# Sums of weight quarters made on GpSimd during the attention, from each converted piece, and stored beside it

## The chip, the cores and the metric

The program runs on one core of a Trainium2 chip. The metric is the time of one execution on the device in microseconds. A core has TensorE (matrix products, "PE" in the profile; its weight loads are "PEld"), VectorE ("DVE"), ScalarE ("ACT"), GpSimd ("POOL") and SyncE ("SP", here the queue from which nearly all transfers are issued).

## The reference

Three blocks follow each other. The attention works on 8 batches with 8 heads, 576 positions and 64 features; the mixer and the MLP work on 8 x 576 positions of 512 features.

```
phi(x): p = x @ w_phi; p = p - max|p|; concat(exp(p), exp(-p))
attention: (phi(q) @ (phi(k)^T v)) / (phi(q) . sum phi(k) + 1e-6)
gate = sigmoid(causal 5-tap convolution of x, per feature)
x = (gate * (x @ w_val)) @ w_out
u = x + real(FFT over positions and features of x)
un = layer norm of u
out = u + relu(un @ w_ch1) @ w_ch2
```

The weights w_val, w_out, conv_w, w_ch1 (512 x 2048) and w_ch2 (2048 x 512) come as 64-bit floats and are converted to 32 bits on the chip.

## The kernel before

Three phases follow each other. The attention (to about 312 us) is written out by hand in steps (`run_attention`): 16 units of two heads each, five groups of positions per unit, 80 steps in all. In each step TensorE projects (pj), transposes (yt, xt), accumulates phi(k)^T v (kv) and applies it (nm); VectorE takes maxima from PSUM (m, L260) and subtracts them (y, L263); ScalarE takes the exponentials (ke, qe). Finished heads go to DRAM by SP's queue (x_scr<-xT, L362).

Beside these steps 21 weight pieces are converted (`convert`), 16 of them of the two MLP weights (`conv_mlp`). A piece is loaded (raw, L121), ScalarE converts the low word, VectorE makes three passes (L133, L134 and the scalar_tensor_tensor into mt), ScalarE makes the exponent (L137) and the sign (L139), and GpSimd multiplies twice (L140, L141) in place in mt, a buffer of which there are two. Two places later `done` issues the store of mt from SP's queue (L378). The places of one piece lie 0, 3, 4, 5, 6 and 8 steps after its start, and a piece starts every 3.1 steps on average. Small tables are loaded through a tile tab between these steps.

A piece of an MLP weight is four quarters of 128 x 256 (a21, a11, a12, a22). The MLP multiplies 2 x 2 blocks with seven products instead of eight, and needs for it four sums of these quarters besides: s22 = a21 + a22, s21 = a11 - a21, s11 = s22 - a11, s12 = a12 - s11. Slots 0 to 3 of the scratch s_scr hold the quarters, slots 4 to 7 the sums.

Mixing (312 to about 620 us) and MLP are not written out by hand. Functions note operations with their costs and keys (`o_tt`, `o_lo`, `o_dma`, ...), and a planner (`place_ops`) puts all of them in one order, with due times from the products backwards; operations marked "vp" may go to VectorE or to GpSimd, whichever the planner finds better. In the mixing, `note_sums` loads a piece back from DRAM into one buffer ws, makes the four sums in place on GpSimd and stores them; a table SUMS says after which products each of the 16 pieces is noted. When the attention's pools are closed, `open_mix2` opens the second mixing stage's tiles and clears some of them on GpSimd (L453): c256, r256, xr, rem. The mixing computes val (x @ w_val), the taps (acc), gv and gs (gated values), ge (their two parts), ps (w_out and the Fourier products), and two halves of a first layer norm (s, sl, A, T).

All operations issued through helpers carry L62, so rows are told apart by their tiles. Products are made of a high and a low part, so many operations come in pairs: ScalarE writes the high part, VectorE or GpSimd the rest (xh, ge, f, sl).

Of the kernel before, what the change touches and what calls it, by code (L numbers as in the profile page):

```python
# [9 lines left out]
F32 = mybir.dt.float32  # L10
# [13 lines left out]
NE = HS + 2  # L24
# [41 lines left out]
def attention_moe_mixer_kernel(  # L66
# [46 lines left out]
        mm(o, al, bh, start=False, stop=last)  # L113


    def convert(i, src, n, shape, halve, done):
        raw = P["xf"].tile([128, 1024, 2], I32, tag="xf", name="raw64")[:, 0:n]
        raw_k = raw.rearrange("p n t -> p (n t)").rearrange("p (k f) -> p k f", k=shape[0])
        if shape[0] == 8:
            for o in range(2):  # L120
                nc.sync.dma_start(out=raw_k[:, o::2], in_=src[o])  # L121
        else:
            nc.sync.dma_start(out=raw_k, in_=src)
        yield
        lo32, hi32 = raw[:, :, 0].bitcast(U32), raw[:, :, 1]
        a = P["xh"].tile([128, 2, 1024], I32, tag=f"x{i % 2}", name="cv")
        ex, lo = a[:, 0, 0:n], f32(a[:, 1, 0:n])
        sg = lo
        mt = stg.tile([128, 1024], I32, tag="mt", name="mt")[:, 0:n]
        w = f32(mt)  # L130
        nc.scalar.activation(out=lo, in_=lo32, func=ACTF.Copy, scale=2.0 ** -32)
        yield
        nc.vector.tensor_scalar(out=mt, in0=hi32, scalar1=0xFFFFF, scalar2=0x4B000000, op0=ALU.bitwise_and, op1=ALU.bitwise_or)  # L133
        nc.vector.tensor_scalar(out=ex, in0=hi32, scalar1=0x7FF00000, scalar2=None, op0=ALU.bitwise_and)  # L134
        vec.scalar_tensor_tensor(out=w, in0=w, scalar=-7340032.0, in1=lo, op0=ALU.add, op1=ALU.add)
        yield
        nc.scalar.activation(out=ex, in_=ex, func=ACTF.Relu, scale=8.0, bias=ebias[:, int(halve):int(halve) + 1])  # L137
        yield
        nc.scalar.activation(out=sg, in_=hi32, func=ACTF.Sign)  # L139
        nc.gpsimd.tensor_tensor(out=w, in0=w, in1=f32(ex), op=ALU.mult)  # L140
        nc.gpsimd.tensor_tensor(out=w, in0=w, in1=sg, op=ALU.mult)  # L141
        yield
        done(w.rearrange("p (k f) -> p k f", k=shape[0]))
        yield
# [3 lines left out]
    def later(k, *at):  # L148
        def get():
            t = late[k]  # L150
            for i in at:
                t = t[i]
            return t
        return Late(get)
# [48 lines left out]
    y_p = pool(early, "y", 2, side=R)  # L203
    stg = pool(early, "stg", 2, side=R)
    vraw_p = pool(early, "vraw", 2, side=R)
    ps_pj = pool(early, "ps_pj", 2, PSUM, side=R)
    ap1 = pool(att, "ap1", 1)
    qe_p = pool(att, "qe", 4)
# [164 lines left out]
    def slices(i, j, q):  # L373
        return s_scr[i][j // (i + 1)][q, :, j % (i + 1)].rearrange("q p o f -> p q (o f)")

    def conv_mlp(n, j, i):
        def done(t):
            nc.sync.dma_start(out=slices(i, j, slice(0, 4)), in_=t.rearrange("p (q o) f -> p q (o f)", o=2))  # L378
        s = (w_ch1, w_ch2)[i][j].bitcast(I32).rearrange("o p (q f) -> o p q f", q=4)
        return convert(n, s, 1024, (8,), False, done)  # L380

    def note_sums(n):
        i, j = wsteps[n]
        t = later("ws")
        a21, a11, a12, a22 = (t[:, k] for k in range(4))
        k21, k11, k12, k22 = keys = [("ws", k) for k in range(4)]
        o_dma([(t, slices(i, j, slice(0, 4)))], [], keys, 512)
        o_tt("p", a22, a21, a22, ALU.add, 256, [k21, k22], [k22])
        o_tt("p", a21, a11, a21, ALU.subtract, 256, [k11, k21], [k21])
        o_tt("p", a11, a22, a11, ALU.subtract, 256, [k22, k11], [k11])  # L390
        o_tt("p", a12, a12, a11, ALU.subtract, 256, [k12, k11], [k12])
        o_dma([(slices(i, j, slice(4, 8)), t)], keys, [("s", i, j)], 512)

    def conv_taps(i):
        def done(t):
# [2 lines left out]

    def put_table(dst, src):
        r, n = src.shape  # L400
        t = stg.tile([128, 580], F32, tag="tab", name="tab")
        nc.sync.dma_start(out=t[0:r, 0:n], in_=src)
        yield
        hi_act(dst, t[0:r, 0:n])
        yield
# [12 lines left out]

    def open_mix():
        p = pool(gx, "g0", 1, side=R)  # L420
        ws = pool(vx, "ws", 1, side=R)
        psv = pool(vx, "psv", 1, PSUM, side=R)
        psa = pool(vx, "psa", 1, PSUM, side=R)
        for g, q in enumerate((p, P["g1"])):
            for i in range(2):
                late["ge", g, i] = q.tile([128, 4, 2, NE], F32R, tag=f"g{i}", name="ge")
        for i in range(2):
            late["pv", i] = psv.tile([128, NE + 2], F32, name=f"val{i}")
            late["gv", i] = P["g"].tile([128, NE], F32, tag="gv", name="gv")
            late["gs", i] = P["g"].tile([128, 2, NE], F32, tag="gs", name="gs")  # L430
        late["ws"] = ws.tile([128, 4, 256], F32, name="ws")
        late["pa"] = psa.tile([128, 2, 512], F32, name="acc")

    def open_mix2():
# [20 lines left out]
    def open_last():  # L455
# [4 lines left out]
        for i in (4,):  # L460
            late["ps", i] = ps.tile([128, 512], F32, name=f"ps{i}")
        open_mlp()

    wsteps = [(i, j) for j in range(NJ) for i in range(2)]

    def load_x(b):
        t = P["xf"].tile([128, 4, S + 4], F32, tag="xf", name="xf")
# [213 lines left out]
    def note_weights(c, n, first=[]):  # L681
        per = (7 * NJ, 7 * NJ // 2)[c]
        t, r = divmod(n, per)
        if t == len(BLOCKS):
            return
        j, i = divmod(r, 7)
        s = (f"r{c}", n % RING[c])
        w = later(s)
        hk, lk = s + (0,), s + (1,)
        cols = (256, 512)[c]  # L690
        h, l = (w[:, k].rearrange(("p k f -> p (k f)", "p n k f -> p (n k f)")[c]) for k in range(2))
        q = SLOT[ORDER[c][i]]
        src = s_scr[c][j][q].rearrange("p n k f -> p (n k f)")
        o_dma([(f32(l), src)], [("s", c, x) for x in ((j,), (2 * j, 2 * j + 1))[c] if q > 3] + first + (over(s) if c == 0 and n < RING[0] else []), [lk], (128, 256)[c])
        o_hi(h, f32(l), cols, [lk], [hk])
        o_lo(K["w"], l, f32(l), h, cols, [lk, hk], [lk])

# [251 lines left out]
    def note_W(b, c):  # L949
        gh, gl = (later(("ge", b % 2, k)) for k in range(2))  # L950
        w = int(b == NB - 1)
        t = later(("x2", w))
        fs, f = tl["fs"], [later(("f", i)) for i in range(2)]
        for a in range(2):
            k, p = next(ring)
            p = p[:, 0:NE]

            def prod(e, a=a, p=p):
                for kk in range(4):
                    ws = slice(c * 128, (c + 1) * 128)  # L960
                    mm3(p, (wo[0][:, kk, ws], wo[1][:, kk, ws]), (gh[:, kk, a], gl[:, kk, a]), kk == 0, kk == 3)
            op("m", 0, prod, [("ge", b % 2, kk, i) for kk in range(4) for i in range(2)] + ["wo"], [k] + [("done", "W", c, a)] * (b == NB - 2), 12 * 0.134)
            if c >= 2:
                o_tt("v", fs[:, a], t[:, c - 2, a], p, (ALU.add, ALU.subtract)[a], NE, [k, ("x2", w, c - 2, a)], [("fs", a)])
            if c == 2 and a == 0:
                r = later(("xr", b % 2))
                o_hi(r[0:1], p[0:1], NE, [k], [("xr", b % 2, 0)])
                o_lo("v", r[32:33], p[0:1], r[0:1], NE, [k, ("xr", b % 2, 0)], [("xr", b % 2, 1)])
            o_act(t[:, c, a], p, ACTF.Copy, NE, [k] + [("s",) + wsteps[-1]] * w, [("x2", w, c, a)])
        if c >= 2:  # L970
            c0 = c - 2
            fk = [("fs", 0), ("fs", 1)]
            o_hi(f[0][:, c0], fs, 2 * NE, fk, [("f", c0, 0)])
            o_lo(K["t_lo"], f[1][:, c0], fs, f[0][:, c0], 2 * NE, fk + [("f", c0, 0)], [("f", c0, 1)])
        if c == 2:
            q0 = 32 * (b % 4)
            o_act(later("r256")[q0:q0 + 1], t[0:1, 2], ACTF.Copy, 2 * NE, [("x2", w, 2, 0), ("x2", w, 2, 1)], [("r256", b % 4)])
# [79 lines left out]
    def note_mix():  # L1057
        rings = [[(("ps", i), later(("ps", i))) for i in range(n)] for n in (4, 5)]
        nonlocal ring
        ring = cycle(rings[0])  # L1060
        sums = iter(range(len(wsteps)))
        SUMS = [(1, 0, 1, 0, 1)] * 5 + [(1, 0, 0, 0, 0), (0,) * 5]

        def add_sums(n):
            for i in range(n):
                k = next(sums, None)
                if k is not None:
                    in_place(note_sums, k)

        ln0 = chain(ln_first(0), ln_first(1))  # L1070
        tail = note_tail()
        next(tail)
# [4 lines left out]
        for b in range(NB - 1):  # L1077
            note_x(b + 1)
            for i, c in enumerate((0, 2, 1, 3)):
                if i < 3:  # L1080
                    note_taps(b + 1, i)
                    note_V(b + 1, i)
                note_W(b, c)
                add_sums(SUMS[b][i])
            add_sums(SUMS[b][4])
            note_taps(b + 1, 3)
            note_V(b + 1, 3)
            if b == NB - 2:
# [440 lines left out]
```

## Time and profile before

| | |
|---|---|
| median of 3 runs | 1338.03 us (1337.85 to 1338.59) |
| profiled execution, own time | 1339.93 us |
| its span, first to last instruction | 1338.1 us |
| TensorE busy | 1302.2 us (97%) |
| VectorE busy | 1186.8 us (89%) |
| ScalarE busy | 925.5 us (69%) |
| GpSimd busy | 699.2 us (52%) |
| granted TensorE clock, mean | 0.998 of full speed |

Busy shares are averages over phases that differ; what bounds a phase is read in its own stretch. A stall of TensorE in one phase isn't made good in another, since the phases follow each other and each needs the one before. The rows of the profile give start and duration in microseconds from the span's start, and behind an arrow what ended an engine's idle time.

### The profile page before, as it was taken

How to read it: one execution, taken by the hardware profiler on the slowest of the kernel's cores; microseconds unless marked ns; L12 is line 12 of the kernel's file. 1: busy time of each engine (PE TensorE's matmuls, PEld its weight loads, DVE VectorE, ACT ScalarE, POOL GpSimd, SP SyncE). 2: the span in 40 equal slices, each digit the busy share in tenths (PEclk: the TensorE clock that was granted, in tenths of full speed). 3: DMA queues.
4: the chain of work that ended last, by engine and by line, in shares of the span. 5: the costliest groups of instructions: out<-in, count | busy, mean ns of one | idle time of the engine just before them, and what ended most of it. 6: DMA issues, size and time to landing. Idle time of an engine off the chain costs nothing.

```text
span 1338.1 us, 30770 instructions
## 1 busy us (share of the span) xinstructions
PE 1302.2 (97%) x11952; PEld 1188.0 (89%) x11952; DVE 1186.8 (89%) x1900; ACT 925.5 (69%) x1874; POOL 699.2 (52%) x599
## 2 busy tenths in 40 slices
PE   8999999999899998999999999999999999999998
PEld 7888888888899998998888888888888888889997
DVE  7999999989898998979998998898889989888875
ACT  6888888866555546565877686777777676776662
POOL 1534343404467566536655774488457945583321
PEclk9999999999999999999999999999999999999999
DMA  7578878643344453334633463347333743345322
GB/s 273 172 264 275 277 260 289 209 180 118 116 150 147 134 161 111 124 121 155 219 104 102 155 220 108 98 135 240 108 102 103 231 144 103 107 142 182 106 86 88
DMA packets 151598, 214.63 MB, mean 160 GB/s; under 512 B 16790, under 2 KB 112278, under 8 KB 151452
## 3 DMA queue, kind: packets, MB, share of 16 engines
q1 hardware_dynamic: 146992, 203.05, 47.5%
q10 hardware_dynamic: 4460, 9.62, 1.9%
q8 instruction: 94, 1.54, 0.5%
q14 instruction: 52, 0.43, 0.1%
HBM read 165.63 MB, written 46.99 MB: 159 GB/s over the span
## 4 chain that ended last, share of the span: by engine, by line
PE 74%; DVE 18%; DMA 2%; ACT 2%; issue 2%; POOL 1%; SPq 0%; DVEq 0%; POOLq 0%; ACTq 0%
PE x L62 15%; PE cx L62 15%; PE cy L62 11%; PE ps L62 10%; PE y L62 8%; PE val L62 4%; PE z L62 4%; DVE y L263 3%; DVE m L260 3%; DVE acc L62 2%; PE kv L62 2%; PE pj L62 2%; PE nm L62 2%; DVE mt L62 2%; PE yt L313 1%
## 5 line engine op out<-in xcount | busy, mean ns | idle before, releaser
L62 POOL TENSOR_TENSOR r<-r 128x256 fp32r<-128x256 f32 (+1 forms) x301 | 292.6, 989 | 242.8 <-ACT r L62 228.7
L62 PE MATMUL x<-un,r 128*128 128x462 f32 (+1 forms) x960 | 221.7, 372 | 2.2 <-ACT c L62 1.4
L62 ACT ACTIVATE r<-r 128x256 fp32r<-128x256 f32 (+1 forms) x420 | 193.2, 486 | 42.0 <-DMA r<-s_scr 40.7
L62 PE MATMUL cx<-h,r 128*128 128x462 f32 (+1 forms) x960 | 213.9, 371 | 1.1 <-DVE acc L62 1.1
L62 PEld LDWEIGHTS x<-un,r 128*128 128x128 f32 x960 | 180.3, 188 | 23.9 <-DVE c L62 1.9
L62 PEld LDWEIGHTS cx<-h,r 128*128 128x128 f32 x960 | 180.3, 188 | 22.1 <-DVE acc L62 1.9
L62 PE MATMUL cy<-h,r 128*128 128x462 f32 (+1 forms) x720 | 160.2, 371 | 0.0
L62 PEld LDWEIGHTS cy<-h,r 128*128 128x128 f32 x720 | 135.4, 188 | 15.3
L62 PE MATMUL val<-xh,wv 128*128 128x290 f32 x768 | 116.5, 300 | 9.2 <-DVE gv L62 4.5
L62 PEld LDWEIGHTS val<-xh,wv 128*128 128x128 f32 x768 | 106.6, 189 | 13.1 <-DVE gv L62 6.2
L62 PE MATMUL y<-un,r 128*128 128x462 f32 (+1 forms) x480 | 113.6, 371 | 0.0
L62 DVE SCALAR_TENSOR_TENSOR acc<-xf,cw,acc 128x576 f32<-128x576 f32 x128 | 105.0, 824 | 8.2 <-ACT acc L62 7.6
L62 PE MATMUL ps<-ge,wo 128*128 128x290 f32 x768 | 108.1, 297 | 2.2 <-DVE fs L62 1.4
L62 PEld LDWEIGHTS ps<-ge,wo 128*128 128x128 f32 x768 | 104.7, 189 | 3.2 <-DVE fs L62 1.6
L140 POOL TENSOR_TENSOR mt<-mt,cv 128x1024 f32<-128x1024 f32 (+1 forms) x21 | 47.5, 2263 | 105.8 <-ACT cv L137 101.6
L62 PEld LDWEIGHTS y<-un,r 128*128 128x128 f32 x480 | 90.2, 188 | 10.3
L62 DVE TENSOR_TENSOR acc<-cx,acc 128x924 f32<-128x924 f32 (+1 forms) x80 | 88.8, 1110 | 11.7 <-PE cx L62 9.7
L260 DVE TENSOR_REDUCE m<-pj 128x8 f32<-128x1024 f32 (+1 forms) x80 | 88.6, 1108 | 9.3 <-PE pj L62 9.3
L62 PE MATMUL kv<-vraw,ke 128*64 128x66 f32 x2560 | 93.4, 225 | 1.2 <-DVE kvT L305 0.5
L62 PE MATMUL pj<-wp,kqraw 64*128 64x128 f32 x1152 | 87.9, 290 | 5.0 <-DMA kqraw<-in_k_dram 4.7
L62 PEld LDWEIGHTS kv<-vraw,ke 128*64 128x64 f32 x2560 | 81.7, 137 | 11.7 <-ACT ke L272 1.1
L62 ACT ACTIVATE h<-z 128x462 fp32r<-128x462 f32 (+1 forms) x120 | 66.4, 553 | 34.9 <-DVE z L62 31.1
(176 smaller groups left out, 2809.5 us busy)
## 6 DMA issues: line engine op xcount, KB each, us to landing
r<-s_scr SPq DMA_DIRECT2D x280, 128.0 KB, 2.2
r<-s_scr SPq DMA_DIRECT2D x140, 256.0 KB, 2.6
raw<-in_w_ch_dram SPq DMA_DIRECT2D x32, 512.0 KB, 5.9
vraw<-in_v_dram SPq DMA_DIRECT2D x16, 660.0 KB, 9.3
x_scr<-xT SPq DMA_DIRECT2D x32, 288.0 KB, 2.3
xf<-x_scr SPq DMA_DIRECT2D x8, 1152.0 KB, 6.5
u_scr<-u ACTq DMA_DIRECT2D x8, 1152.0 KB, 4.5
kqraw<-in_k_dram SPq DMA_DIRECT2D x15, 576.0 KB, 5.6
```

What stands on the lines that cost most here:

```text
L62: return lambda *a, **k: f(*(resolve(x) for x in a), **{n: resolve(x) for n, x in k.items()})
L140: nc.gpsimd.tensor_tensor(out=w, in0=w, in1=f32(ex), op=ALU.mult)
L260: nc.vector.tensor_reduce(out=m, in_=pv, axis=AX.X, op=ALU.max, apply_absolute_value=True)
L263: nc.vector.tensor_tensor(out=y, in0=pv, in1=m.unsqueeze(3).to_broadcast([128, 2, 2 * n, F]), op=ALU.subtract)
L313: nc.tensor.transpose(t[:, h, j, :], y[:, h, n + j, :], ident)
```

## The change

The four sums of an MLP piece are now made by GpSimd directly behind its two multiplications, from the converted quarters in mt, into a tile s of which there is one. At the piece's last place SP issues two stores, mt and s. `note_sums`, its loads, the tile ws, the table SUMS and the keys by which weight loads and the last batch's results waited for the sums are gone. The tile tab moves from the pool of mt, which has two buffers, into that of s, which has one.

```diff
-    def convert(i, src, n, shape, halve, done):
+    def convert(i, src, n, shape, halve, done, also=None):
...
         nc.gpsimd.tensor_tensor(out=w, in0=w, in1=sg, op=ALU.mult)
+        if also:
+            also(w.rearrange("p (k f) -> p k f", k=4))
         yield
...
+    sums_p = pool(early, "sums", 1, side=R)
...
     def conv_mlp(n, j, i):
...
-    def note_sums(n):
-        i, j = wsteps[n]
-        t = later("ws")
-        a21, a11, a12, a22 = (t[:, k] for k in range(4))
...
-        o_dma([(t, slices(i, j, slice(0, 4)))], [], keys, 512)
-        o_tt("p", a22, a21, a22, ALU.add, 256, [k21, k22], [k22])
...
-        o_dma([(slices(i, j, slice(4, 8)), t)], keys, [("s", i, j)], 512)
+        t = {}
+
+        def sums(w):
+            t["w"], t["s"] = w, sums_p.tile([128, 4, 256], F32, tag="s", name="s")
+            a21, a11, a12, a22 = (w[:, k] for k in range(4))
+            s21, s11, s12, s22 = (t["s"][:, k] for k in range(4))
+            nc.gpsimd.tensor_tensor(out=s22, in0=a21, in1=a22, op=ALU.add)
+            nc.gpsimd.tensor_tensor(out=s21, in0=a11, in1=a21, op=ALU.subtract)
+            nc.gpsimd.tensor_tensor(out=s11, in0=s22, in1=a11, op=ALU.subtract)
+            nc.gpsimd.tensor_tensor(out=s12, in0=a12, in1=s11, op=ALU.subtract)
+
+        def done(_):
+            for q, x in enumerate((t["w"], t["s"])):
+                nc.sync.dma_start(out=slices(i, j, slice(4 * q, 4 * q + 4)), in_=x)
...
-        t = stg.tile([128, 580], F32, tag="tab", name="tab")
+        t = sums_p.tile([128, 580], F32, tag="tab", name="tab")
...
-        ws = pool(vx, "ws", 1, side=R)
...
-                add_sums(SUMS[b][i])
-            add_sums(SUMS[b][4])
```

On GpSimd in the attention, where the first two pieces of the MLP weights are multiplied, the order before was:

```order
L141 TENSOR_TENSOR mt<-mt,cv 128x20
L396 COPY cw<-mt 128x20
L140 TENSOR_TENSOR mt<-mt,cv 128x1024
L141 TENSOR_TENSOR mt<-mt,cv 128x1024
L140 TENSOR_TENSOR mt<-mt,cv 128x1024
L141 TENSOR_TENSOR mt<-mt,cv 128x1024
```

And it is now, at the same place:

```order
L140 TENSOR_TENSOR mt<-mt,cv 128x1024
L141 TENSOR_TENSOR mt<-mt,cv 128x1024
L386 TENSOR_TENSOR s<-mt 128x256
L387 TENSOR_TENSOR s<-mt 128x256
L388 TENSOR_TENSOR s<-s,mt 128x256
L389 TENSOR_TENSOR s<-mt,s 128x256
L140 TENSOR_TENSOR mt<-mt,cv 128x1024
L141 TENSOR_TENSOR mt<-mt,cv 128x1024
```

Four sums stand behind each L141, and the next piece's L140 behind them.

On SP's queue in the attention, around one of the pieces (s_scr_1_84 is its scratch, x_scr the finished heads, raw the next piece's 64-bit words), the order is now:

```order
L405 DMA tab<-in_feat_tab_dram 128x516
L393 DMA s_scr_1_84<-mt 128x4x256
L393 DMA s_scr_1_84<-s 128x4x256
L365 DMA x_scr_67<-xT 128x576
L365 DMA x_scr_68<-xT 128x576
L121 DMA raw_3324<-in_w_ch_dram 128x4x256 x2
L237 DMA kqraw<-in_k_dram 128x1152
```

The store of s is the only new row; it stands between the store of mt and the stores of xT.

On GpSimd at the opening of the mixing, the order before was:

```order
L62 TENSOR_TENSOR xh<-xf,xh 128x576 x4
L62 TENSOR_TENSOR ws<-ws 128x256 x8
L62 TENSOR_TENSOR ge<-gs,ge 128x580
L62 TENSOR_TENSOR xh<-xf,xh 128x576
L62 TENSOR_TENSOR ws<-ws 128x256 x7
L453 MEMSET c_6043 128x640
L453 MEMSET r_6044 97x580
L453 MEMSET xr_6047 128x290
```

It is now:

```order
L62 TENSOR_TENSOR xh<-xf,xh 128x576 x4
L62 TENSOR_TENSOR ge<-gs,ge 128x580
L62 TENSOR_TENSOR xh<-xf,xh 128x576
L454 MEMSET c_6117 128x640
L454 MEMSET r_6118 97x580
L454 MEMSET xr_6121 128x290
```

Fifteen sums ahead of the memsets are gone, and the rest keeps its order.

## Rows read from the trace of the kernel before

**Rows 1.** Stretch, us, busy of PE PEld DVE ACT POOL, clock, DMA share, GB/s.

```profile
45.00:310.00 265.00, 256.89 (x5532) 229.44 (x5532) 244.21 (x432) 216.31 (x418) 96.79 (x46) 1.00 0.70 235
310.00:360.00 50.00, 44.11 (x428) 40.90 (x424) 44.73 (x92) 25.87 (x45) 20.41 (x25) 1.00 0.36 116
...
500.00:530.00 30.00, 25.70 (x174) 24.40 (x173) 26.75 (x45) 16.27 (x29) 18.27 (x18) 0.95 0.32 110
```

**Rows 2.** Chain of work, 45 to 310 us: shares by line.

```profile
by line: DVE y L263 12.1%; DVE m L260 11.8%; PE kv L62 11.6%; PE nm L62 11.0%; PE pj L62 11.0%; DVE mt L62 6.4%; PE yt L313 5.8%; issue 5.4%; DVE mt L133 4.6%; DVE xs L342 3.9%; DMA s_scr<-mt 3.6%; DVE r L341 2.5%; PE xt L355 2.1%; DVE kvT 
```

**Rows 3.** VectorE's groups, 45 to 310 us: busy us, mean ns, idle before.

```profile
L62 DVE SCALAR_TENSOR_TENSOR mt<-mt,cv 128x1024 f32<-128x1024 f32 x17 | 20.6, 1214 | 0.0
L133 DVE TENSOR_SCALAR mt<-raw 128x1024 int32<-128x1024 int32 x17 | 15.3, 903 | 0.0
```

**Rows 4.** Chain of work, 308 to 362 us: start us, us, what.

```profile
327.26 7.25 DMA s_scr<-ws
...
339.06 0.74 POOL ws L62
339.80 0.07 issue
...
342.25 2.91 DMA s_scr<-ws
...
352.87 0.40 ACT xr L62
```

**Rows 5.** Waits, 310 to 360 us: total us, times, longest us.

```profile
ACT xr L62 <- POOL xr L453: 4.5, 1, 4.5
...
DVE fs L62 <- ACT x L62: 3.5, 1, 3.5
PE val L62 <- DVE gv L62: 3.3, 2, 2.1
```

**Rows 6.** GpSimd's groups over the span: the sums.

```profile
L62 POOL TENSOR_TENSOR ws<-ws 128x256 f32<-128x256 f32 x64 | 52.4, 818 | 36.1 <-DMA ws<-s_scr 31.5 <-DVE xs L342 1.9
```

**Rows 7.** Timeline of SP's queue: the last store of xT.

```profile
340.07 0.33 SPq L678 DMA_DIRECT2D x_scr<-xT  x1
```

**Rows 8.** Timeline, 312 to 315 us: tap passes and sums.

```profile
312.17 1.36 DVE L62 SCALAR_TENSOR_TENSOR acc<-xf,cw,acc 128x576 f32<-128x576 f32 x1 [0.85 <-ACT acc L62]
...
314.17 1.54 DVE L62 SCALAR_TENSOR_TENSOR acc<-xf,cw,acc 128x576 f32<-128x576 f32 x2
314.20 1.38 POOL L62 TENSOR_TENSOR ws<-ws 128x256 f32<-128x256 f32 x1
```

**Rows 9.** Timeline of GpSimd, 155 to 165 us: one piece and the next.

```profile
155.19 2.38 POOL L141 TENSOR_TENSOR mt<-mt,cv 128x1024 f32<-128x1024 f32 x1 [2.65 <-ACT cv L139]
163.11 2.36 POOL L140 TENSOR_TENSOR mt<-mt,cv 128x1024 f32<-128x1024 f32 x1 [5.54 <-ACT cv L137]
```

**Rows 10.** Stores of mt: KB and median us to landing; one issue.

```profile
s_scr<-mt SPq DMA_DIRECT2D x16, 512.0 KB, 8.7
...
160.39 0.54 SPq L378 DMA_DIRECT2D s_scr<-mt  x1
```

**Rows 11.** Timeline: L141 and the next piece's L133, early and late; another L133.

```profile
82.69 2.38 POOL L141 TENSOR_TENSOR mt<-mt,cv 128x1024 f32<-128x1024 f32 x1 [2.75 <-ACT cv L139]
...
85.60 0.69 DVE L133 TENSOR_SCALAR mt<-raw 128x1024 int32<-128x1024 int32 x1
...
169.83 0.68 DVE L133 TENSOR_SCALAR mt<-raw 128x1024 int32<-128x1024 int32 x1
...
238.61 2.37 POOL L141 TENSOR_TENSOR mt<-mt,cv 128x1024 f32<-128x1024 f32 x1 [2.73 <-DVE kvT L305]
...
241.53 0.68 DVE L133 TENSOR_SCALAR mt<-raw 128x1024 int32<-128x1024 int32 x1
```

**Rows 12.** Timeline, 105 to 108 us: L133 that meets L141.

```profile
105.19 2.37 POOL L141 TENSOR_TENSOR mt<-mt,cv 128x1024 f32<-128x1024 f32 x1 [1.71 <-ACT cv L139]
...
106.58 1.53 DVE L133 TENSOR_SCALAR mt<-raw 128x1024 int32<-128x1024 int32 x1
```

More of the change, by code (lines that the diff above doesn't have):

```diff
@@ L376, in conv_mlp @@
     def conv_mlp(n, j, i):
[L377 to L380, printed above, removed]
-    def note_sums(n):
-        i, j = wsteps[n]
-        t = later("ws")
-        a21, a11, a12, a22 = (t[:, k] for k in range(4))
-        k21, k11, k12, k22 = keys = [("ws", k) for k in range(4)]
-        o_dma([(t, slices(i, j, slice(0, 4)))], [], keys, 512)
-        o_tt("p", a22, a21, a22, ALU.add, 256, [k21, k22], [k22])
-        o_tt("p", a21, a11, a21, ALU.subtract, 256, [k11, k21], [k21])
-        o_tt("p", a11, a22, a11, ALU.subtract, 256, [k22, k11], [k11])
-        o_tt("p", a12, a12, a11, ALU.subtract, 256, [k12, k11], [k12])
-        o_dma([(slices(i, j, slice(4, 8)), t)], keys, [("s", i, j)], 512)
+        t = {}
[10 more added lines that the diff above has]
+                nc.sync.dma_start(out=slices(i, j, slice(4 * q, 4 * q + 4)), in_=x)
+        src = (w_ch1, w_ch2)[i][j].bitcast(I32).rearrange("o p (q f) -> o p q f", q=4)
+        return convert(n, src, 1024, (8,), False, done, sums)
     def conv_taps(i):
@@ L430, in open_mix @@
             late["gs", i] = P["g"].tile([128, 2, NE], F32, tag="gs", name="gs")
-        late["ws"] = ws.tile([128, 4, 256], F32, name="ws")
         late["pa"] = psa.tile([128, 2, 512], F32, name="acc")
@@ L462, in open_last @@
         open_mlp()
-    wsteps = [(i, j) for j in range(NJ) for i in range(2)]
     def load_x(b):
@@ L693, in note_weights @@
         src = s_scr[c][j][q].rearrange("p n k f -> p (n k f)")
-        o_dma([(f32(l), src)], [("s", c, x) for x in ((j,), (2 * j, 2 * j + 1))[c] if q > 3] + first + (over(s) if c == 0 and n < RING[0] else []), [lk], (128, 256)[c])
+        o_dma([(f32(l), src)], first + (over(s) if c == 0 and n < RING[0] else []), [lk], (128, 256)[c])
         o_hi(h, f32(l), cols, [lk], [hk])
@@ L968, in note_W @@
                 o_lo("v", r[32:33], p[0:1], r[0:1], NE, [k, ("xr", b % 2, 0)], [("xr", b % 2, 1)])
-            o_act(t[:, c, a], p, ACTF.Copy, NE, [k] + [("s",) + wsteps[-1]] * w, [("x2", w, c, a)])
+            o_act(t[:, c, a], p, ACTF.Copy, NE, [k], [("x2", w, c, a)])
         if c >= 2:
@@ L1060, in note_mix @@
         ring = cycle(rings[0])
[L1061 to L1068, printed above, removed]
         ln0 = chain(ln_first(0), ln_first(1))
```

## The prediction

> **What bounds the kernel now.** I read the stretch table first [rows 1]. Four parts matter. In the attention (45 to 310 us) TensorE is busy 256.9 of 265 us and VectorE 244.2: two engines share the bound. In the opening of the mixing (310 to 360) TensorE loses 5.9 of 50 us while VectorE is busy 44.7. From 500 to 530 TensorE loses 4.3 us and its granted clock averages 0.95. So time can be gained in the opening and around 515.
>
> The chain of work through the attention [rows 2] puts VectorE's passes over each converted weight piece on the path: the first (L133) 4.6% and the third 6.4% of 265 us, 29.2 us together, against 15.3 + 20.6 = 35.9 us of busy time for these two groups [rows 3]. So about 0.81 of a microsecond lost there reaches the end.
>
> The chain through the opening of the mixing [rows 4] runs through the work that the change takes away: a store of sums (7.25 us to landing), the load of the next piece, its sums from 339.06 on, their store (2.91), one more load with three sums, and behind them on GpSimd the memsets of the second mixing stage. The list of waits [rows 5] shows who pays: ScalarE waits 4.5 us for the memset of xr, VectorE 3.5 us for ScalarE behind it, and TensorE at longest 2.1 us for VectorE's gv.
>
> **What the change removes.** In the mixing go 64 sums of 0.818 us, 52.4 us of GpSimd's time [rows 6], 16 loads and 16 stores on SP's queue. GpSimd is not a bound there, and TensorE never waits for it directly, so only the stall above counts. In the new order the memsets follow directly on an xh split, with no sum and no load ahead. They still need the attention's pools closed. The last store of xT is issued at 340.07 [rows 7]; by the 2.91 us of the store above it lands by 343.0, and six memsets of 0.6 us or less end by 346.6, before ScalarE asks (352.87 [rows 4] less the wait of 4.5, so 348.3). The stall goes. Its worth lies between 2.1 us (TensorE's own idle time) and 3.5 us (VectorE's, which is the busier engine here); I take 3.0. Before that, VectorE's first tap pass takes 1.36 us beside a sum [rows 8], where two passes in a row took 1.54: 0.59 us too long, of which I count 0.5. Together -3.5 us.
>
> The planner, with GpSimd free, also re-places work: three xh splits move to GpSimd, and a ge split, two sl, an s and a u move to VectorE, two instructions more for VectorE in all, and the second LN half is placed earlier against the products. Nothing in the trace prices a new order. I take 0 and bound it by the idle time that is there: -4.3 if the loss from 500 to 530 goes, and as a loss the 3.0 that the opening gave.
>
> **What it adds.** Each of the 16 pieces gets four sums and a store of 512 KB in the attention. In the opening's chain an undisturbed sum takes 0.74 us and the next starts 0.07 us later [rows 4]: 0.81 each, 3.2 us for four.
>
> GpSimd has the room: L141 ends at 157.57, and the next L140 starts after 5.54 us of idle time [rows 9], 2.3 us more than the sums need. The single buffer s must have been stored before the next piece's sums start: sums 3.2, landing 8.7 (the median of the stores beside it [rows 10]), 0.4 for the issue: 12.3 us, against 12.0 from L141 to L141 (82.69 to 238.61, 13 pieces on [rows 11]). So GpSimd waits a little at some pieces, and the 2.3 us cover that. If SP comes late by more than that, the pieces queue up behind this buffer. On SP's queue the s store stands behind the mt store and waits for the last sum; kqraw, vraw, raw and xT stand behind it. These already wait on this queue for ScalarE, so I cost the block at nothing; without that cover it is up to 3.2 us a piece.
>
> VectorE is where it can hurt. Its three passes over the next piece start shortly after L141 ends: 0.53 us after at the first pair (85.07 to 85.60) and 0.55 at one of the last (240.98 to 241.53) [rows 11]. Of the 15 pairs, eight start 0.18 to 0.82 us after, five before or within 0.04 us, two later than 3.5 us. The sums now fill just this gap. What a pass loses when it meets GpSimd's work is seen in rows: L133 at 106.58 took 1.53 us instead of 0.69, held until L141 ended [rows 12]. A sum that begins 0.07 us after L141 ends 0.81 us after it, so the eight pairs lose 0.81 us less their own distance each: 0.28, 0.13, 0.35, 0, 0.02, 0.31, 0.63, 0.26, together 2.0 us. Whether the second and third pass lose another sum each is not shown for these passes. Below, they lose nothing: in the opening two tap passes back to back took 1.54 us with a sum running, and it was the sum that was stretched, to 1.38 us [rows 8]. Above, thirteen pairs lose two sums more each, 13 x 2 x 0.74 = 19.2 us. The tap passes have the same operation as the third pass and follow their predecessor in the same way, so I take the lower end. On the path 2.0 x 0.81 = 1.6 us.
>
> The Trainium skill (SBUF — State Buffer, "Who interferes with whom") says that a VectorE instruction with two SBUF inputs or in a two-port mode and a GpSimd instruction exclude each other for the whole instruction. The trace agrees for the pass that comes second (1.53 and 1.36 us) and not for the pair of 1.54 us, which ran beside a sum. By the page's rule alone the upper end above would hold; it stands behind the slower rival below.
>
> The stores add 16 x 512 KB = 8.4 MB to 265 us x 235 GB/s = 62 MB [rows 1], 13%; an 8.7 us landing becomes 1.1 us later. A pass L133 must wait until the mt store of two pieces before has landed; at the tightest, 160.39 + 8.7 = 169.1 against L133 at 169.83 [rows 10, 11], 0.7 us in hand. So 0.4 us late at perhaps two pieces: 0.7 us. Bounds 0 and 15 x 0.4 = 6.
>
> From the first products of the MLP on, TensorE, VectorE and ScalarE have the same order as before; I count 0.
>
> **The sum.** -3.5 + 1.6 + 0.7 = -1.2 us. The profiled execution took 1339.93 us, so 1338.7 as profiled. That execution lies 1.90 us above the median of the three runs (1338.03), so 1336.8 there.
>
> **The rivals.**
> Faster, 1333.0: VectorE's passes lose nothing because the sums arrive second, and the idle time of 500 to 530 shrinks with the new placement. For it: VectorE leads in bursts, and the opening stall is on the chain. Against it: the products around that LN half stand in nearly the same order as before. -3.5 for the opening, -2.0 of the 4.3, and +0.5 for late landings: -5.0, 1333.0 against the median.
> Slower, 1344.6: each of thirteen pieces loses one more sum on VectorE, 13 x 0.74 x 0.81 = 7.8 us, so -1.2 + 7.8 = +6.6. For it: 80% of the passes' time is on the chain, and four sums come one after another. Against it: the burst of [rows 8]. From 0.55 us per piece on (-3.5 + 13 x 0.55 x 0.81 + 0.7 = +3.0) it decides.
> No gain, 1339.8: the memsets come early, but ScalarE then waits for something as late, and 0.5 of the 3.5 is left: -0.5 + 2.3 = +1.8. Against it: the 5.3 us in hand from 343.0 to 348.3.
>
> **How the numbers follow.** Chances: the forecast 0.36, the faster case 0.34, the slower 0.24, no gain 0.06. What differs by less than 0.2%, 2.7 us, is no change to a measurement of this kernel: the forecast and "no gain" lie within, so 0.34 faster, 0.42 same, 0.24 slower. The range reaches from 1331.5 (the faster case with 1.5 us more of the 500 to 530 loss) to 1342.5, which leaves out the worse half of the slower case and the tail of the faster, below 0.2. The forecast's own range is 1334.5 to 1339.
>
> **What would show it.** Right: ScalarE's wait for the xr memset is gone and TensorE is busy 46.5 us or more in the fifty that now hold the opening; L133's mean rises from 0.903 us to about 1.0, and the third pass stays at 1.21; the attention ends 1 to 3 us later. Wrong: L134 and the third pass grow too (exclusion), GpSimd idles for the s store, L133 waits for a DMA, or the loss near 500 to 530 has moved or gone, which I have set to no change.

## The result, and the profile after

The changed kernel takes 1345.57 us (median of four runs, 1344.52 to 1346.21) where the kernel before takes 1337.94 beside it: a ratio of 1.0059, 95% interval 1.0041 to 1.0076. On a second chip the ratio was 1.0040 (1.0026 to 1.0054). It is slower by 5 to 8 us; the prediction said 1336.8 and ended its range at 1342.5.

The phases follow each other, so I measured each by start times in the traces. "Attention" is from the fifth maximum pass (m) on VectorE to the eightieth and last, "mixing" from the first product val to the first product x of the MLP, "MLP" from there to the end. "Start" is the fifth maximum pass itself.

| trace | start at | attention | mixing | MLP | span |
|---|---|---|---|---|---|
| before | 19.0 | 288.2 | 305.8 | 719.9 | 1338.1 |
| before, second profile | 20.6 | 289.3 | 305.0 | 719.9 | 1340.1 |
| after | 20.2 | 303.4 | 293.5 | 721.4 | 1343.9 |
| after, second profile | 21.4 | 303.1 | 293.6 | 721.2 | 1344.5 |

So a loss of 14 to 15 us in the attention stands against a gain of 11 to 12 in the mixing. I had predicted +2.3 and -3.5. The start varies by 1 to 2 us between executions of either kernel, and the MLP is 1.4 us longer. Added up, the traces give 4.4 to 5.8 us for the whole span; the medians on the two chips give 5.4 and 7.6.

Busy time and the stretches (stretch, us, busy of PE PEld DVE ACT POOL, clock, DMA share, GB/s), which answer to [rows 1]; the first val stands 16.5 us later than there, the end of the mixing 4 us:

```profile
PE 1301.5 (97%) x11952; PEld 1188.5 (88%) x11952; DVE 1199.3 (89%) x1902; ACT 924.3 (69%) x1874; POOL 714.9 (53%) x597
```

```profile
45.00:326.00 281.00, 258.42 (x5545) 230.27 (x5542) 260.37 (x434) 217.26 (x419) 166.29 (x110) 1.00 0.74 253
326.00:376.00 50.00, 46.88 (x467) 44.39 (x463) 47.25 (x98) 28.96 (x51) 7.04 (x10) 1.00 0.17 55
504.00:534.00 30.00, 29.38 (x219) 28.97 (x218) 28.99 (x54) 17.50 (x33) 14.96 (x11) 1.00 0.21 72
```

TensorE now idles 22.6 of 281 us in the attention where it idled 8.1 of 265, while VectorE is busy 16.2 us more. In the opening of the mixing TensorE is busy 46.9 of 50 us (44.1 before), and the loss near the end of the mixing (25.7 of 30) is gone.

The groups of VectorE's three passes over a piece in the attention (busy us, mean ns, idle before), to be set beside [rows 3]:

```profile
L62 DVE SCALAR_TENSOR_TENSOR mt<-mt,cv 128x1024 f32<-128x1024 f32 x17 | 27.7, 1631 | 0.0
...
L134 DVE TENSOR_SCALAR cv<-raw 128x1024 int32<-128x1024 int32 x17 | 18.9, 1109 | 0.0
L133 DVE TENSOR_SCALAR mt<-raw 128x1024 int32<-128x1024 int32 x17 | 16.4, 964 | 0.0
```

L134 before:

```profile
L134 DVE TENSOR_SCALAR cv<-raw 128x1024 int32<-128x1024 int32 x17 | 11.7, 686 | 0.0
```

L133 rose from 903 to 964 ns, where I had said about 1.0 us. But L134 rose from 686 to 1109 ns and the third pass from 1214 to 1631: 1.1 + 7.2 + 7.1 = 15.4 us of busy time, as much as the whole loss of the attention. The means hide two kinds of pieces: in 13 of the 17 L134 takes 1.23 to 1.25 us and the third pass 1.75 to 1.77, about 0.55 us more each, and in the other four neither loses anything. GpSimd's sums are stretched too, against the 0.74 us of an undisturbed one [rows 4]:

```profile
L388 POOL TENSOR_TENSOR s<-s,mt 128x256 f32<-128x256 f32 x16 | 21.8, 1364 | 0.0
L387 POOL TENSOR_TENSOR s<-mt 128x256 f32<-128x256 f32 x16 | 17.3, 1084 | 0.0
L389 POOL TENSOR_TENSOR s<-mt,s 128x256 f32<-128x256 f32 x16 | 15.5, 970 | 1.3
L386 POOL TENSOR_TENSOR s<-mt 128x256 f32<-128x256 f32 x16 | 15.0, 939 | 3.6 <-DMA s_scr<-s 2.6
```

How this comes about is seen in the timeline of one piece, VectorE first, then GpSimd (start us, us, what); [rows 11, 12] showed the same place before:

```profile
110.05 1.51 DVE L133 TENSOR_SCALAR mt<-raw 128x1024 int32<-128x1024 int32 x1
111.47 1.24 DVE L134 TENSOR_SCALAR cv<-raw 128x1024 int32<-128x1024 int32 x1
112.63 1.76 DVE L62 SCALAR_TENSOR_TENSOR mt<-mt,cv 128x1024 f32<-128x1024 f32 x1
```

```profile
108.62 2.38 POOL L141 TENSOR_TENSOR mt<-mt,cv 128x1024 f32<-128x1024 f32 x1 [2.77 <-ACT cv L139]
111.08 1.08 POOL L386 TENSOR_TENSOR s<-mt 128x256 f32<-128x256 f32 x1
112.12 1.18 POOL L387 TENSOR_TENSOR s<-mt 128x256 f32<-128x256 f32 x1
113.27 1.72 POOL L388 TENSOR_TENSOR s<-s,mt 128x256 f32<-128x256 f32 x1
115.06 0.72 POOL L389 TENSOR_TENSOR s<-mt,s 128x256 f32<-128x256 f32 x1
```

In this piece the two engines take turns. L133 waits for L141 to end; the first sum then waits for L133, L134 for the first sum, the second sum for L134, the third pass for the second sum, the third sum for the third pass. Only the fourth sum, with no pass left, takes its 0.72 us. The chain of waits files nearly all of a held L134 under "issue": 12 pieces show an "issue" of 1.01 to 1.03 us there, ahead of the third pass.

The memsets, which stood behind fifteen sums [rows 4, 5], now follow an xh split at once, 21.5 us after the first val (328.96; before, 38.9 us after it), and ScalarE's wait for xr is gone:

```profile
348.85 1.66 POOL L62 TENSOR_TENSOR xh<-xf,xh 128x576 fp32r<-128x576 f32 x1 [0.60 <-ACT xh L62]
350.44 0.63 POOL L454 MEMSET c<- 128x640 f32 x1
...
351.53 0.63 POOL L454 MEMSET xr<- 128x290 f32 x2
```

SP's queue has a new wait (queue, line, what it waited for: us, times, longest), and in the chain of waits one of its ends is a load of V (start us, us, what):

```profile
SPq L393 <- POOL s L389: 41.3, 12, 4.5
```

```profile
169.93 0.56 POOL s L389
...
170.51 0.38 SPq L393
...
170.98 7.15 DMA vraw<-in_v_dram
```

The last sum releases the store of s, and vraw is issued 0.47 us behind it; the chain goes on from there, 7.15 us later, with VectorE's y.

### The profile page after: what moved, and what is told of

Same layout as the page of the kernel before. It is cut to its first block, busy times and chain, and to the rows that moved or that the text cites. A ratio compares the mean times of both kernels' runs of the same rounds, so it can differ in the third digit from the quotient of the medians.

```text
span 1343.9 us, 30769 instructions
## 1 busy us (share of the span) xinstructions
PE 1301.5 (97%) x11952; PEld 1188.5 (88%) x11952; DVE 1199.3 (89%) x1902; ACT 924.3 (69%) x1874; POOL 714.9 (53%) x597
## 4 chain that ended last, share of the span: by engine, by line
PE 76%; DVE 18%; issue 2%; DMA 2%; ACT 2%; SPq 0%; POOL 0%; DVEq 0%; POOLq 0%; ACTq 0%
PE cx L62 14%; PE x L62 14%; PE ps L62 12%; PE cy L62 10%; PE y L62 7%; PE val L62 6%; PE z L62 4%; DVE y L266 3%; DVE m L263 3%; DVE mt L62 2%; DVE acc L62 2%; PE kv L62 2%; PE nm L62 2%; PE pj L62 2%; DMA vraw<-in_v_dram 2%
## 5 line engine op out<-in xcount | busy, mean ns | idle before, releaser
L62 PE MATMUL nm<-kvT,qe 128*64 128x65 f32 x2304 | 82.2, 222 | 14.6 <-DVE xs L345 14.2
L62 PEld LDWEIGHTS nm<-kvT,qe 128*64 128x64 f32 x2304 | 74.6, 138 | 17.6 <-issue 14.9
```

The source lines that it names most:

```text
L62: return lambda *a, **k: f(*(resolve(x) for x in a), **{n: resolve(x) for n, x in k.items()})
```

## The experiments

Ratios are against the kernel before on the same chip, and the passes' lengths are means of 17; its median varied from 1337.9 to 1341.9 us between chips, so times are not compared across runs. "Attention" is the length defined above.

| run | ratio to before (95%) | attention, us | L133, L134, third pass, us |
|---|---|---|---|
| before, two profiles | 1 | 288.2, 289.3 | 0.90, 0.69, 1.21 |
| after, two profiles | 1.0059, 1.0040 | 303.4, 303.1 | 0.96, 1.11, 1.63 |
| neither sums nor store | 0.9925 (0.9910 to 0.9940) | 288.5 | 0.94, 0.69, 1.22 |
| store of a fixed tile, no sums | 0.9930 (0.9907 to 0.9952) | 289.0 | 0.94, 0.69, 1.22 |
| store of the piece, no sums | 0.9956 (0.9939 to 0.9972) | 293.9 | 0.92, 0.69, 1.22 |
| sums, no store | 1.0022 (1.0009 to 1.0035) | 302.2 | 0.96, 1.11, 1.63 |
| sums in halves | 0.9981 (0.9965 to 0.9997) | 296.2 | 0.96, 0.89, 1.42 |
| sums between L140 and L141 | 1.0076 (1.0061 to 1.0091) | 308.9 | 1.77, 0.68, 1.21 |
| sums behind the third pass | 0.9953 (0.9935 to 0.9971) | 294.2 | 0.91, 0.69, 1.22 |
| the same, no store | 0.9923 (0.9897 to 0.9949) | 290.6 | 0.90, 0.69, 1.22 |
| the same, store from GpSimd late | 1.0203 (1.0176 to 1.0229) | 328.1 | 1.39, 1.88, 1.21 |
| the same, store from GpSimd at once | 0.9959 (0.9946 to 0.9973) | 293.4 | 0.99, 0.69, 1.22 |
| after, store from GpSimd | 1.0026 (1.0015 to 1.0037) | 301.3 | 0.97, 1.01, 1.53 |

**One part at a time.** Four runs take the sums and the store of s apart: the store with the piece itself in place of s, the sums without a store, neither, and a store of a tile that is set once. All four leave the sums out of the program's result, so they are timings and not kernels to use. The edit for "no store" is:

```diff
-            for q, x in enumerate((t["w"], t["s"])):
+            for q, x in enumerate((t["w"],)):
...
-        src = s_scr[c][j][q].rearrange("p n k f -> p (n k f)")
+        src = s_scr[c][j][q % 4].rearrange("p n k f -> p (n k f)")
```

> The changed kernel without the four sums: the piece itself is stored a second time in place of s (the sums are left out of the result), so that all DMA traffic stays and GpSimd's new work goes. Theory 1: passes at 0.90, 0.69 and 1.21 us, first xh split at 295 to 298 us, time 1328 to 1332. Theory 2: attention still 8 us or more late, time 1338 to 1347.

> The changed kernel with the four sums but without the store of s (weight loads of the MLP read the four stored quarters in place of the sums, which are left out of the result): GpSimd's new work stays, the extra 8.4 MB and the queue's wait for the sums go. Theory 1: passes at about 0.96, 1.11 and 1.63 us as in the changed kernel, first xh split at 311 to 313 us, time 1344 to 1346. Theory 2: first xh split at 296 to 304 us, time 1330 to 1338.

> The changed kernel with neither the sums nor the store of s (weight loads as in the run with the sums alone; the sums are left out of the result): the kernel before without its sums in the mixing. Both theories: first xh split at 295 to 297 us and the mixing as fast as in the changed kernel, so about 1338 - 12 + 1.5 = 1327 to 1330. Theory 1: within 1.5 us of the run with the store alone. Theory 2: 8 us or more below it.

> The changed kernel without the four sums, and with the second store of each piece taken from a tile that is set once (the sums are left out of the result): traffic alone, with nothing on SP's queue waiting for GpSimd and no second hold on the piece's buffer. In the run that stored the piece twice, VectorE waited 3.8 us at L133, for the buffer. If that hold made the 4.7 us between that run and the one with neither: 0 to 2 us above the run with neither (0.9925 to 0.994 of the kernel before). If the traffic itself did: 4 us or more above it (0.9955 or more).

The attention says it plainly: 288.5 us with neither, 302.2 with the sums alone, 289.0 with the traffic alone, 303.4 and 303.1 with both. The sums cost 13.7 us. The traffic's 0.5 is less than two executions of the kernel before differ by (1.1), so it can't be told from nothing. The run that stored the piece twice had 293.9: there VectorE idles 3.8 us ahead of L133, which writes the buffer that the second store still reads, and the changed kernel doesn't idle there; with the fixed tile, which frees that buffer, the 5 us are gone, so they belong to the experiment. The store beside the sums is worth about 1 us by the traces (303.4 and 303.1 less 302.2); the ratios, 1.0059 and 1.0040 against 1.0022, would make it 5 and 2.4 us, each uncertain by 2 us or more. Its price there stays open.

**Half as long a sum.** Each sum became two of 128x128 at the same place.

```diff
-            nc.gpsimd.tensor_tensor(out=s22, in0=a21, in1=a22, op=ALU.add)
...
+                for c in (slice(0, 128), slice(128, 256)):
+                    nc.gpsimd.tensor_tensor(out=o[:, c], in0=x[:, c], in1=y[:, c], op=alu)
```

> The changed kernel with each sum of 128x256 split into two of 128x128 at the same place (eight instructions a piece). Theory 1 (a pass of VectorE waits for the one GpSimd instruction in progress, and they take turns): a half takes about 0.47 us instead of 0.74 (from 0.74 for 256 and 2.37 for 1024 columns), so each of L134 and the third pass loses about 0.27 us instead of 0.42, to 0.96 and 1.48 us, and 3 to 6 us of the attention come back. Rival (each meeting costs a fixed hand-over, whatever the length): means stay at 1.11 and 1.63 us or grow, time not below that of the changed kernel (1.0059 of the kernel before).

```profile
L62 DVE SCALAR_TENSOR_TENSOR mt<-mt,cv 128x1024 f32<-128x1024 f32 x17 | 24.1, 1420 | 0.0
...
L134 DVE TENSOR_SCALAR cv<-raw 128x1024 int32<-128x1024 int32 x17 | 15.2, 893 | 0.0
```

L134 and the third pass lose 0.21 us each on average instead of 0.42: the loss follows the length of the GpSimd instruction that is met, and is no fixed price of a meeting. Seven of 15 us come back with twice the instructions.

**The sums elsewhere, first try.** Between the next piece's L140 and L141, where GpSimd waits for ScalarE's sign.

```diff
         nc.gpsimd.tensor_tensor(out=w, in0=w, in1=f32(ex), op=ALU.mult)
+        if held:
+            held.pop()()
         nc.gpsimd.tensor_tensor(out=w, in0=w, in1=sg, op=ALU.mult)
```

> The changed kernel with the sums of a piece issued on GpSimd between the next piece's L140 and L141 (where GpSimd waits for ScalarE's sign) instead of right behind its own L141, and the store of s one piece later; the same instructions and the same bytes. Theory 1 (each sum and each of VectorE's three passes over the next piece shut each other out, one after the other): the three passes return to about 0.90, 0.69 and 1.21 us, the first xh split on GpSimd comes back from 312.6 us to 296 to 299, and the time falls by about 15 us to 1329 to 1333. Theory 2 (the second store of 512 KB a piece and its wait on SP's queue hold up the loads): the attention ends as late as in the changed kernel and the time stays at 1342 to 1347. Theory 3 (the sums slow any VectorE work they meet, whatever it is): some 8 us come back, 1336 to 1340.

```profile
L133 DVE TENSOR_SCALAR mt<-raw 128x1024 int32<-128x1024 int32 x17 | 30.1, 1771 | 3.4 <-POOL s L393 3.3
```

None of the three theories held. L134 and the third pass were free, as theory 1 wanted, but GpSimd also waited 28.6 us for the store of s, L141 came later, and L133 then met L141: 0.87 us more on average over 17 pieces, 14.8 us of the 20 that the attention lost. The sums had only been exchanged for a longer instruction in the same place.

**The sums behind the third pass.** A copy of one column of the third pass's result holds them back until the passes are over; the store follows in that step.

```diff
+        if held:
+            nc.gpsimd.tensor_copy(out=gate, in_=w[:, 0:1])
+            store_s = held.pop()()
         nc.gpsimd.tensor_tensor(out=w, in0=w, in1=f32(ex), op=ALU.mult)
         nc.gpsimd.tensor_tensor(out=w, in0=w, in1=sg, op=ALU.mult)
+        if store_s:
+            store_s()
```

> The changed kernel with the sums of a piece held back until VectorE's third pass over the next piece is done (a copy of one column of that pass's result stands ahead of them on GpSimd), between that pass and the next L140; the store of s follows in the same step. Theory 1 (sums and passes shut each other out; the run that put the sums between L140 and L141 failed because L141 came later and L133 waited for all of it, 1.77 us instead of 0.90): now nothing on GpSimd runs while the three passes do, so 0.90 to 0.95, 0.69 and 1.21 us, first xh split at 297 to 301 us, and the time 5 to 9 us below that of the kernel before on the same chip. Rival: wherever the sums stand, GpSimd's 3 us more per piece push L140 and L141 into the next passes; then L133 is again over 1.3 us and the time is at or above that of the kernel before.

Timeline of one piece, VectorE, then GpSimd:

```profile
123.06 0.68 DVE L133 TENSOR_SCALAR mt<-raw 128x1024 int32<-128x1024 int32 x1
123.66 0.69 DVE L134 TENSOR_SCALAR cv<-raw 128x1024 int32<-128x1024 int32 x1
124.26 1.23 DVE L62 SCALAR_TENSOR_TENSOR mt<-mt,cv 128x1024 f32<-128x1024 f32 x1
```

```profile
125.55 0.19 POOL L141 COPY gate<-mt 128x1 f32<-128x1 f32 x1 [3.98 <-DVE mt L62]
125.69 0.73 POOL L395 TENSOR_TENSOR s<-mt 128x256 f32<-128x256 f32 x1
...
127.89 0.74 POOL L398 TENSOR_TENSOR s<-mt,s 128x256 f32<-128x256 f32 x1
128.59 2.37 POOL L145 TENSOR_TENSOR mt<-mt,cv 128x1024 f32<-128x1024 f32 x1
```

The passes are back at 0.91, 0.69 and 1.22 us with the same 64 sums in the attention: theory 1 is shown, since the sums cost what they did by where they stood. At 0.9953 this version beats both kernels (1334.19 us against 1339.69 on its chip). Its attention is still 5 to 6 us longer than the kernel before's.

**What is left there: the store's place.** The same without the store, then with the store issued from GpSimd's own queue, once behind L141 and once directly behind the last sum; and the changed kernel with its store moved to that queue.

```diff
-            nc.sync.dma_start(out=slices(i, j, slice(4, 8)), in_=t["s"])
+            nc.gpsimd.dma_start(out=slices(i, j, slice(4, 8)), in_=t["s"])
```

> The run with the sums held behind the third pass, without the store of s (weight loads of the MLP read the four stored quarters in place of the sums, which are left out of the result). If the store's place on SP is what was left: 0.992 to 0.994 of the kernel before, first xh split at 297 to 300 us. If the sums' own place still costs (L140 and L141 later, ScalarE and VectorE waiting for them): 0.995 or more and first xh split at 301 us or later.

> The run with the sums held behind the third pass, its store of s issued from GpSimd's own queue instead of SP's. If what was left of the loss there (attention 7.5 us later than in the kernel before, 2.3 with the fixed tile) is SP standing at the store of s (38 us in 12 waits) with vraw and raw loads behind it: 2 to 5 us below that run, 0.992 to 0.994 of the kernel before. Rival: GpSimd pays for the issue, or the traffic itself is what costs: no gain, 0.995 or more.

> The run with the sums held behind the third pass, with the store of s issued from GpSimd's own queue directly behind the last sum, ahead of the next L140 (in the run before it stood behind L141, so the next sums waited 74 us for it). If SP's stand at the store is what the held sums still cost (1.5 to 4 us): attention 2 to 4 us later than in the kernel before, 0.991 to 0.994 of it. If the issue on GpSimd (0.91 us each) pushes L141 into the next L133: L133 over 1.1 us and 0.996 or more.

> The changed kernel with the store of s issued from GpSimd's own queue. Theory: sums against passes make about 13 us and the block of SP's queue 1.5 to 5: 1.0022 to 1.005 of the kernel before, the passes as in the changed kernel (0.96, 1.11, 1.63 us). Rival (the block is hidden behind the stretched passes): no change, 1.0045 to 1.007.

> The changed kernel, unchanged, on this chip: 1.004 to 1.0075 of the kernel before. If the store costs 4 us or more beside the sums, 1.0055 or more (the run without it had 1.0022, the one with GpSimd's queue 1.0026); if it costs about 1.5 us, 1.003 to 1.0045.

Without the store the attention falls from 294.2 to 290.6 us: the store costs 3.6 us where the passes no longer hide it. Its bytes alone had cost about 0.5, so I put most of that down to its place. This run, too, leaves the sums out of the result. In the changed kernel GpSimd's queue takes 2 us off the attention (301.3). Part of that is not SP's: the sums now wait at times (7.9 us for the store of s) and meet fewer passes: L134 fell to 1.01 and the third pass to 1.53. Behind the third pass, GpSimd's queue gains nothing at once (0.9959 against 0.9953): SP no longer waits, but the issue takes 0.80 us of GpSimd, and L133 rises to 0.99. Behind L141 it was a blunder of mine: the store went out so late that the next sums waited 74.2 us for it, and L134 rose to 1.88 us on meeting L141:

```profile
POOL s L395 <- DMA s_scr<-s: 74.2, 15, 7.0
```

The changed kernel, run again, came at 1.0040, within what I had expected for a store that costs about 1.5 us beside the sums. How the 3.6 us divide between SP's wait (38.1 us in 12) and GpSimd's for the single buffer (4.3 us) stays open.

**The mixing.** One run moves the table of sums a batch later, one takes the memsets of xr and rem off GpSimd and moves nothing else, and one is the kernel before again.

```diff
-        SUMS = [(1, 0, 1, 0, 1)] * 5 + [(1, 0, 0, 0, 0), (0,) * 5]
+        SUMS = [(0,) * 5] + [(1, 0, 1, 0, 1)] * 5 + [(1, 0, 0, 0, 0)]
```

```diff
-            nc.gpsimd.memset(f32(late[k]), 0.0)
+            (nc.vector if k[0] in ("xr", "rem") else nc.gpsimd).memset(f32(late[k]), 0.0)
```

> The kernel before with the sums in the mixing one batch later (none in the first batch, so none stands ahead of the memsets of the second mixing stage). If the stall at the memsets is what the mixing gains (my step of the prediction): ScalarE's wait for the xr memset goes and 2 to 4 us are gained against the kernel before, the rest of the mixing unchanged. If most of the 12 us come from the sums' absence everywhere (VectorE and planner): gain of 0 to 4 in the opening, and the losses between 360 and 530 us stay or move, total within 4 us of the kernel before either way; above it, if the later sums now fall into the narrow place at 500 to 530 us.

> The kernel before, all sums in the mixing, with the four memsets of xr and rem on VectorE instead of GpSimd; every other instruction keeps its place. If the stall at the memsets is worth what I put down for it: ScalarE's wait for xr (4.5 and 4.7 us in two profiles of the kernel before) goes and the time falls by 2 to 3.5 us, less about 1 us for VectorE's four instructions; mixing 303 to 304 us from the first val to the first x (305.8 and 305.0 before, 293.5 in the changed kernel). Rival: the next thing on the way is as late, and the stall is worth less than 1 us: mixing at 305 us or above, time within 1 us of the kernel before or above it.

> The kernel before, unchanged, for a second profile of it. In its first profile TensorE keeps its full clock at 11 to 15 us, where every run since shows a stretch at 0.5 and a loss of 1.5 to 2 us, and loses 4 us and clock at 510 to 530. If the first belongs to the change, it is absent here too; if it comes and goes with the execution, the loss of 1.5 to 2 us is here as well. The loss at 510 to 530 should be here.

In the kernel before again the granted clock stays at 1.00 from 11 to 15 us, as it does in the changed kernel's second profile, and it falls to 0.50 there in the run with the memsets on VectorE: it comes and goes with the execution. The loss at 500 to 530 is there.

Stretches of the kernel before again, the memsets on VectorE, and the later table, each opening (the first val at 315, 313 and 314 us) and 500 to 530 us:

```profile
312.00:362.00 50.00, 44.61 (x432) 41.63 (x433) 44.73 (x91) 25.38 (x43) 21.75 (x26) 0.97 0.37 122
500.00:530.00 30.00, 26.07 (x185) 24.76 (x183) 26.69 (x49) 14.61 (x27) 18.90 (x18) 1.00 0.35 120
```

```profile
312.00:362.00 50.00, 46.27 (x435) 43.71 (x434) 48.56 (x101) 29.24 (x51) 20.77 (x22) 1.00 0.42 129
500.00:530.00 30.00, 25.74 (x186) 24.39 (x185) 26.75 (x48) 18.43 (x35) 18.39 (x18) 1.00 0.30 108
```

```profile
312.00:362.00 50.00, 46.52 (x422) 43.36 (x423) 45.76 (x94) 27.01 (x47) 20.04 (x25) 0.97 0.38 114
500.00:530.00 30.00, 28.52 (x213) 27.82 (x213) 28.94 (x54) 19.58 (x40) 16.11 (x16) 1.00 0.29 99
```

With the memsets on VectorE, ScalarE's wait for xr is gone and the mixing takes 301.9 us in the trace: 3.1 to 3.9 us less, more than the 1 to 3 expected, with the loss at 500 to 530 untouched. The timed runs don't confirm it as a gain (0.9995, 0.9986 to 1.0004); that profile's execution, at 1337.57, lies 1.75 us below the median of its runs. So the stall is shown to go, and what it is worth in the time stays open between 0 and about 2 us here. The later table missed its aim, since the planner kept the first fifteen sums ahead of the memsets. But TensorE's order differs from about 447 us on, the loss at 500 to 530 falls from 3.9 to 1.5 us, the mixing is 5.6 to 6.4 us shorter (299.4), and the kernel takes 0.9961 of before, with all 64 sums still in the mixing. Of that, 0.9 to 2.0 us are gained ahead of 447 us, in an unchanged order (ScalarE's wait for xr is 2.5 us there instead of 4.5 and 4.7), and 3.6 to 5.5 behind it. So a new order alone can bring such a gain, without the sums' absence; that the changed kernel's own new order does the same is argued from this, not shown.

## Why the prediction was wrong, point by point

**The step that failed: "The tap passes have the same operation as the third pass and follow their predecessor in the same way, so I take the lower end."** The term that I set to nothing measured 7.2 us at L134 and 7.1 at the third pass. The upper end that I had written down, 13 x 2 x 0.74 = 19.2, was the nearer one: its thirteen pieces and two sums were right, and each meeting cost 0.55 us instead of 0.74. The slower rival counted one sum more per piece, and it was two. The two tap passes of [rows 8] are not alike. `note_taps` accumulates in the tile sg for the first batch's first two feature blocks and in the PSUM tile pa from the third on, and both carry the name acc. In the trace's operands the pass at 314.17 reads its running total as one row of 576, the next one, at 314.90, as two rows of 288, the shape of pa. GpSimd's sum that began at 314.20 waited out the first (1.38 us) and then ran beside the second, which lost nothing and has one operand in PSUM. The third pass reads and writes SBUF alone. The same trace of the kernel before bears this out over all its tap passes, which have one operation and one size: 72 with the shape of pa that ran beside a GpSimd tensor_tensor for 0.4 us or more took 0.815 us on average, as did the 30 that met none (0.815), while of the eight with one row of 576 two took 1.36 and 1.50 us beside one. This could have been read before the prediction.

The Trainium skill (SBUF — State Buffer, "Who interferes with whom") says that a VectorE instruction with two SBUF inputs, or in a two-port mode, and a GpSimd instruction that reads SBUF exclude each other, and that one with at most one SBUF input outside those modes doesn't contend. The traces agree with both halves: 1.11 and 1.63 us here, 1.215 for the maxima and y. That L134, with its one input, runs in a two-port mode is not named by any trace; it takes 0.69 us for the 1024 columns for which y takes 1.21.

**Share on the chain.** 0.81 was somewhat low: against the run with neither, the sums alone stretched the passes by 14.4 us and the attention by 13.7, 0.95 of it.

**L133's own loss** (2.0 us predicted in eight pairs): 1.1 in all, its mean 0.96 where I said about 1.0. Its mean is 0.94 with neither sums nor store, so what the sums add is less than half of what I said. Too high, but small.

**Landings +0.7 us:** 0.5 by the fixed tile, which fits, but is less than two executions differ by. **The s buffer:** GpSimd waited for it 2.6 us in three places, and behind each of them it still waited 2.8 to 4.9 us for ScalarE, so its slack covered it. Right.

**SP's block at nothing:** about 1 us in the changed kernel's traces and 2.4 to 5 by the ratios, so its size stays open; the store costs 3.6 once the passes are free. I had named the cover (SP waits for ScalarE anyway); it hides most, not all, and a vraw load behind the store reaches the chain at 170.98.

**Opening of the mixing -3.5 us:** TensorE busy 46.9 of 50 us (46.5 or more predicted), the wait for xr gone, and the memsets alone worth 3.1 to 3.9 in the trace. Right in mechanism; the size fits the traces, but the timed gain of the memsets alone can't be told from nothing.

**The planner's re-placement 0, bounds -4.3 to +3.0:** mis-sized, and beyond its bound. The mixing is 11.4 to 12.3 us shorter, so about 8 beyond the stall. The loss at 500 to 530 is gone, and the later table shows that a new order alone can be worth 3.6 to 5.5. The rest, 2.5 to 4 us in small steps between 360 and 490 us, I didn't trace to a cause.

**MLP 0:** 1.4 us longer. Its order is the same, and runs with the changed mixing spread from 719.3 to 723.1. In the profile after, the granted clock falls in the gap of TensorE at the MLP's opening, which the kernel before has too; in the second profile after it stays at 1.00 there and the MLP is as long (721.2), so that isn't the cause, which stays open.

So two terms were mis-sized, the attention by about 12 us and the mixing by about 8 the other way. The difference of about 4 us is about half of the miss (8.8 us, or 6.6 by the second chip's ratio); 1.4 more is the MLP's, about 1 lies in the start, and the rest is between traces and medians. That the slower rival's 1344.6 comes near the measured time is luck: it had 10.1 us of loss in the attention and 3.5 of gain in the mixing, and both were too small.

## What to carry to other kernels

Before you move work to an idle GpSimd, look at what VectorE does just behind the instruction that frees it. Here passes over SBUF alone, one with a single input (L134) and one with two (the third pass), ran in turns with GpSimd's sums, and each pass that met a sum of 0.74 us lost about 0.55 us. Place such work where VectorE works from PSUM, if need be by a dependence that isn't one of data, or split it into short instructions; here the first turned 1.004 to 1.006 into 0.995, and the second into 0.998. When a row is to price an overlap, check where its operands lie, and not only its operation and shape.

## What the runs showed of the hardware

L134 and the third pass, which work in SBUF alone, excluded GpSimd's sums: 1.23 to 1.25 and 1.75 to 1.77 us in the pieces that met them, 0.69 and 1.21 without. VectorE's passes from PSUM ran beside GpSimd's sums without loss on either side. In the profile after, VectorE's y, which reads pj from PSUM, and the sums beside it (VectorE, then GpSimd):

```profile
124.05 1.21 DVE L266 TENSOR_TENSOR y<-pj,m 128x1024 f32<-128x1024 f32 x1
```

```profile
123.98 0.75 POOL L386 TENSOR_TENSOR s<-mt 128x256 f32<-128x256 f32 x1
124.67 0.76 POOL L387 TENSOR_TENSOR s<-mt 128x256 f32<-128x256 f32 x1
```

The granted clock after the same gap differed: in the first 8 us stretch below, the changed kernel's, it averaged 0.81, between the levels of 1.2 and 2.4 GHz, in the kernel before's, the second, 1.00, with TensorE busy 5.84 us in both. In the changed kernel's second profile it stayed at 1.00 too, at the same place and with the same 5.84 us, so it goes with the execution and not with the change.

```profile
630.00:638.00 8.00, 5.84 (x21) 4.51 (x20) 6.71 (x13) 5.75 (x14) 1.90 (x2) 0.81 1.00 353
```

```profile
626.00:634.00 8.00, 5.84 (x27) 4.60 (x26) 6.96 (x13) 6.91 (x16) 1.90 (x2) 1.00 1.03 359
```
